# Emitting the first two mixer groups inside the last column chunk of a long convolution

## The chip, the cores, the metric

The kernel runs on one core of one Trainium2 chip. The metric is the device time of one execution in microseconds (us); lower is better. Each kernel ran several times, and the text quotes medians. A profile shows one further execution, whose span (first to last instruction) is a few us shorter than the timed runs.

The names of the engines in the profile are: PE is the tensor engine (TensorE), DVE is VectorE, ACT is ScalarE, POOL is GpSimd, SP is SyncE (here only a DMA queue). PEclk is the granted clock of TensorE; 1.00 is full speed.

## The reference, cut

Sequence length S = 2048, width D = 1024, MLP width F = 3584, all in bf16.

```python
def A(q, k, v, shift_k, ssm_k, ssm_D):
    kv = (4-tap causal filter of k with shift_k) * v
    y  = irfft(rfft(kv, 2*S) * rfft(ssm_k, 2*S))[:S] + kv * ssm_D   # long convolution over time
    return q * y
def B(x, w1, w2, w3, w4):
    h  = gelu(layernorm(x) @ w1)
    hs = (quarters of h shifted by +1, -1, +2, -2 in time) @ w2
    x1 = x + hs
    return x1 + gelu(layernorm(x1) @ w3) @ w4
x = q
for layer in range(2):
    x = x + A(layernorm(x), k, v, shift_k, ssm_k, ssm_D)
    x = x + B(layernorm(x), w1, w2, w3, w4)
```

The convolution's y depends on k, v and the filters only, not on x. So the kernel computes it once and uses it in both layers.

## The kernel before

**Stage 1** makes y, in four column chunks of 256 channels. In each chunk there are four blocks of time. For block c, TensorE transforms the filter block and the key-value block with a matrix `Fm` (ScalarE evicts them to `Gc`, `Xc`), VectorE makes the products of all pairs of blocks that add up to c (`Za`) and joins neighbours (`Wa`), and TensorE transforms back with `Im`. A store puts y into DRAM (`y_scr`). Block 2 has 3 pairs and block 3 has 4, so VectorE has most to do at the end of a chunk.

**Stage 2** runs 2 layers of 8 groups of 256 rows. For each group: `A_pre` (layer norm, times y, residual, second norm; VectorE with a `pow` on GpSimd), `A_tr` (transposes), `M1` (W1 and gelu), `M2` (W2 with the time shifts), `B_pre` (norm), `B_tr` (transposes), `M34` (W3, gelu, W4: 28 steps f; pieces of the next groups are hooked in at chosen f). "First down-projection" below is the first W4 matmul of group 0: from there on the tensor engine is the limit.

```python
with ExitStack() as p0:                         # stage 1
    cpool = ...                                 # Fm, Im
    with ExitStack() as g0:                     # scratch to compute Fm: kk, prod, pi, rf
        ...
    inp = p0.enter_context(tc.tile_pool(name="p0in", bufs=1))     # knat, hnat, v, kT
    blk, spec, zpool, tpool, wpool0, ypool = ...
    nxt0 = prep0(0)                             # loads k, ssm_k, v of a chunk
    for cc in range(NCH):
        for c in range(NB):
            ...forward transforms, products Za, Wa, inverse transforms...
            nc.gpsimd.dma_start(out=y_t[...], in_=ysb[:])
# p0 is closed here
with ExitStack() as p1:                         # stage 2: its own pools in p0's place
    w3_sb = w3p.tile([P, DT, F], BF16, name="w3_sb")              # 7 MB
    w4p = tile_pool(bufs=4); io = ...; xap = ...; small = ...
    def A_pre(g):
        x_t = io.tile([P, D], BF16, tag="x")
        nc.sync.dma_start(x_t[:], x_src[...])
        y_tile = io.tile([P, D], BF16, tag="y")
        nc.sync.dma_start(y_tile[:], y_scr[...])
        mv = stats(xs)
        nc.gpsimd.tensor_scalar(out=r1[:], in0=mv[:, :, 1], scalar1=EPS, ... op0=ALU.add)
        nc.gpsimd.tensor_tensor(out=r1[:], in0=r1[:], in1=mhalf[:, 0:TPC], op=ALU.pow)
        ...
    for i in range(-3, NG):
        hooks = {}
        ...                                     # W3 and W4 loads at i = -2, -1
        if ok(i + 2): M1(i + 2)                 # hooked at f = 4 when i is 0
        if ok(i + 3): add_hook(hooks, 0, A_pre(i + 3))
        if ok(i + 1): add_hook(hooks, 6 or 1, (M2(i + 1), B_pre(i + 1)))
        if ok(i + 1): add_hook(hooks, 14 or 10, B_tr(i + 1))
        if ok(i + 3): add_hook(hooks, 18, A_tr(i + 3))
        M34(i, hooks)                           # for i < 0: only the hooks, in order of f
```

Of the kernel before, what the change touches and what calls it, by code (L numbers as in the profile page):

```python
# [16 lines left out]
P = 128  # L17
EPS = 1e-5


def _layernorm(nc, small, mhalf, src, dst, D, norm_engine="act"):
    nchunks = (D + 511) // 512
    csz = D // nchunks
    st = small.tile([P, nchunks, 6], FP32, tag="ln_st")
    for i in range(nchunks):
        nc.vector.bn_stats(st[:, i, :], src[:, i * csz:(i + 1) * csz])
    mv = small.tile([P, 2], FP32, tag="ln_mv")
    nc.vector.bn_aggr(mv[:], st[:])
    rstd = small.tile([P, 1], FP32, tag="ln_rstd")
    nc.gpsimd.tensor_scalar(out=rstd[:], in0=mv[:, 1:2], scalar1=EPS, scalar2=None, op0=ALU.add)  # L30
    nc.gpsimd.tensor_tensor(out=rstd[:], in0=rstd[:], in1=mhalf[:], op=ALU.pow)
    if norm_engine == "act":
        nmr = small.tile([P, 1], FP32, tag="ln_nmr")
        nc.vector.scalar_tensor_tensor(out=nmr[:], in0=mv[:, 0:1], scalar=-1.0, in1=rstd[:],
                                       op0=ALU.mult, op1=ALU.mult)
        nc.scalar.activation(out=dst, in_=src, func=AF.Identity, bias=nmr[:], scale=rstd[:])
    else:
        nc.vector.tensor_scalar(out=dst, in0=src, scalar1=mv[:, 0:1], scalar2=rstd[:],
                                op0=ALU.subtract, op1=ALU.mult)
# [3 lines left out]
def kernel(ctx, tc, A_q, A_k, A_v, A_shift_k, A_ssm_k, A_ssm_D, B_x, B_w1, B_w2, B_w3, B_w4, out,  # L43
# [25 lines left out]

    y_scr = tc.dram_tile([S, D], BF16, name="y_scr")  # L70
    y_t = y_scr.rearrange("(t p) d -> p t d", p=P)

# [3 lines left out]
    ident1 = wts12.tile([P, P], BF16, name="ident1")  # L76
    make_identity(nc, ident1[:])
    mhalf = wts12.tile([P, 8], FP32, name="mhalf")
    nc.vector.memset(mhalf[:], -0.5)

    with ExitStack() as p0:
        cpool = p0.enter_context(tc.tile_pool(name="p0c", bufs=1))
        ident = ident1
        Fm = cpool.tile([P, KT, 2, Bs], FP32R, name="Fm")
# [3 lines left out]
        sgn = cpool.tile([P, 2], FP32, name="sgn")  # L88

        with ExitStack() as g0:  # L90
# [17 lines left out]
            for (dst, freev, pc) in ((Fm, kk, pcF),):  # L108
                for j in range(KT):
                    prod = gt.tile([P, 2, Bs], FP32, tag="prod")  # L110
                    nc.vector.tensor_scalar(out=prod[:, 0, :], in0=freev[:], scalar1=pc[:, j:j + 1],
                                            scalar2=float(3 * N // 2), op0=ALU.mult, op1=ALU.add)
                    nc.vector.tensor_scalar(out=prod[:, 1, :], in0=freev[:], scalar1=pc[:, j:j + 1],
                                            scalar2=None, op0=ALU.mult)
                    pi = gt.tile([P, 2, Bs], I32, tag="pi")
                    nc.vector.tensor_copy(pi[:], prod[:])
                    nc.vector.tensor_single_scalar(out=pi[:], in_=pi[:], scalar=2 * N - 1, op=ALU.bitwise_and)
                    rf = gt.tile([P, 2, Bs], FP32, tag="rf")
                    nc.vector.tensor_copy(rf[:], pi[:])
                    nc.scalar.activation(out=dst[:, j, :, :], in_=rf[:], func=AF.Sin, bias=negpi[:],  # L120
                                         scale=math.pi / N)

        inp = p0.enter_context(tc.tile_pool(name="p0in", bufs=1))
        blk = p0.enter_context(tc.tile_pool(name="p0blk", bufs=NB + 1))
        spec = p0.enter_context(tc.tile_pool(name="p0spec", bufs=4))
        zpool = p0.enter_context(tc.tile_pool(name="p0z", bufs=3))
        tpool = p0.enter_context(tc.tile_pool(name="p0t", bufs=3))
        wpool0 = p0.enter_context(tc.tile_pool(name="p0w", bufs=2))
        ypool = p0.enter_context(tc.tile_pool(name="p0y", bufs=2))
        ps_ks = p0.enter_context(tc.tile_pool(name="ps_ks", bufs=3, space=PSUM))  # L130
# [3 lines left out]
        def prep0(cc):  # L134
# [10 lines left out]
            for pc_ in range(npiece):  # L145
                tsl = slice(pc_ * tpp, (pc_ + 1) * tpp)
                nc.sync.dma_start(knat[:, tsl, :], k2.rearrange("(t p) d -> p t d", p=P)[:, tsl, ch0:ch0 + CC])
                nc.sync.dma_start(hnat[:, :, pc_ * tpp * P:(pc_ + 1) * tpp * P],
                                  A_ssm_k[ch0:ch0 + CC, pc_ * tpp * P:(pc_ + 1) * tpp * P].rearrange("(ct p) t -> p ct t", p=P))
                nc.sync.dma_start(v_sb[:, tsl, :], v2.rearrange("(t p) d -> p t d", p=P)[:, tsl, ch0:ch0 + CC])  # L150
# [50 lines left out]
        for cc in range(NCH):  # L201
# [4 lines left out]
            Zprev = None  # L206
            for c in range(NB):
# [19 lines left out]
                if cc == 0 and c == 0:  # L227
                    identf = cpool.tile([P, P], FP32, name="identf")
                    nc.vector.tensor_copy(identf[:], ident[:])
                    for comp in range(2):  # L230
                        for kt in range(KT):
                            pti = ps_fw.tile([P, KT, P], FP32, tag="fw")
                            for j in range(KT):
                                nc.tensor.transpose(pti[:, j, :], Fm[:, j, comp, kt * P:(kt + 1) * P].bitcast(FP32), identf[:])
                            nc.scalar.copy(Im[:, kt, comp, :], pti[:].rearrange("p a b -> p (a b)"))
                a = c
# [29 lines left out]
                for mp in range(KT // 2):  # L266
# [13 lines left out]
                    nc.gpsimd.dma_start(out=y_t[:, t0:t0 + 2, ch0:ch0 + CC], in_=ysb[:])  # L280
# [6 lines left out]
    TC = 256  # L287
    TPC = TC // P
    NCk = S // TC
    NG = 2 * NCk  # L290
    NH = D // 512
    QD = D // 4
    SHIFTS = [1, -1, 2, -2]
    HALO = 2
    nst = (D + 511) // 512
    csz = D // nst
    xa_scr = [tc.dram_tile([S, D], BF16, name=f"xa_scr{l}") for l in range(2)]
    xc_scr = tc.dram_tile([S, D], BF16, name="xc_scr")
    W4P = 4
    assert FT % W4P == 0  # L300
    NPC = FT // W4P
    W4SLOTS = 4

    with ExitStack() as p1:
        w3p = p1.enter_context(tc.tile_pool(name="w3p", bufs=1))
        w3_sb = w3p.tile([P, DT, F], BF16, name="w3_sb")
        w3v = B_w3.rearrange("(kt p) n -> p kt n", p=P)
        w4v = B_w4.rearrange("(kt p) n -> p kt n", p=P)
        W3PIECES = 7 if FT % 7 == 0 else 4
        fs3 = F // W3PIECES  # L310

        def w3_load(i):
            nc.sync.dma_start(w3_sb[:, :, i * fs3:(i + 1) * fs3], w3v[:, :, i * fs3:(i + 1) * fs3])
        w4p = p1.enter_context(tc.tile_pool(name="w4s", bufs=W4SLOTS))
        io = p1.enter_context(tc.tile_pool(name="io", bufs=2))
        xap = p1.enter_context(tc.tile_pool(name="xap", bufs=3))
        xbp = p1.enter_context(tc.tile_pool(name="xbp", bufs=3 * TPC))
        x1p = p1.enter_context(tc.tile_pool(name="x1p", bufs=2 * TPC))
        xlp = p1.enter_context(tc.tile_pool(name="xlp", bufs=2 * TPC))
        small = p1.enter_context(tc.tile_pool(name="small", bufs=6))  # L320
        atp = p1.enter_context(tc.tile_pool(name="aTp", bufs=2))
        btp = p1.enter_context(tc.tile_pool(name="bTp", bufs=2))
        hp = p1.enter_context(tc.tile_pool(name="hTp", bufs=3))
        up = p1.enter_context(tc.tile_pool(name="up", bufs=3))
        ps_s = p1.enter_context(tc.tile_pool(name="ps_side", bufs=2, space=PSUM))
        ps_3 = p1.enter_context(tc.tile_pool(name="ps_3", bufs=2, space=PSUM))
        ps_a = p1.enter_context(tc.tile_pool(name="ps_a", bufs=1, space=PSUM))

        def stats(src_list):
            n = len(src_list)  # L330
            mv = small.tile([P, n, 2], FP32, tag=f"mv{n}")
            for i, src in enumerate(src_list):
                st = small.tile([P, nst, 6], FP32, tag="ln_st")
                for j in range(nst):
                    nc.vector.bn_stats(st[:, j, :], src[:, j * csz:(j + 1) * csz])  # L335
                nc.vector.bn_aggr(mv[:, i, :], st[:])
            return mv

        def lc(g):
            return g // NCk, g % NCk  # L340

        st_aT = {}
        st_a = {}
        st_xb = {}
        st_hT = {}
        st_x1 = {}
        st_b = {}
        st_bT = {}

        def A_pre(g):  # L350
            layer, c = lc(g)
            x_src = q2 if layer == 0 else xc_scr
            xs = []
            ys = []
            for i in range(TPC):
                t = c * TPC + i
                x_t = io.tile([P, D], BF16, tag="x")
                nc.sync.dma_start(x_t[:], x_src[t * P:(t + 1) * P, :])
                y_tile = io.tile([P, D], BF16, tag="y")
                nc.sync.dma_start(y_tile[:], y_scr[t * P:(t + 1) * P, :])  # L360
                xs.append(x_t)
                ys.append(y_tile)
            mv = stats([x[:] for x in xs])
            r1 = small.tile([P, TPC], FP32, tag="r1")
            nc.gpsimd.tensor_scalar(out=r1[:], in0=mv[:, :, 1], scalar1=EPS, scalar2=None, op0=ALU.add)
            nc.gpsimd.tensor_tensor(out=r1[:], in0=r1[:], in1=mhalf[:, 0:TPC], op=ALU.pow)
# [178 lines left out]
        def ok(g):  # L545
            return 0 <= g < NG

# [61 lines left out]
```

## Time and profile before

The time is 1368.26 us (median of 6; 1365.24 to 1370.02).

| stretch of the trace | us | what limits it |
|---|---|---|
| start to first forward transform | 37.7 | TensorE waits for the first loads |
| start of the first forward transform to the end of the last | 217.1 | VectorE's products and TensorE together |
| end of the last forward transform to the first down-projection | 95.9 | VectorE in one chain with short TensorE work |
| first down-projection to the end | 1012.8 | TensorE |

The table of stretches of the kernel before: stretch, its length, busy us of each engine with the number of instructions, then clock, DMA share and GB/s.

```profile
core 0: us, PE busy (x) PEld busy (x) DVE busy (x) ACT busy (x) POOL busy (x), PEclk, DMA share, GB/s
254.80:350.70 95.90, 46.01 (x305) 36.75 (x306) 73.11 (x147) 16.93 (x36) 12.60 (x26) 0.72 0.59 198
350.70:1363.50 1012.80, 996.65 (x7060) 683.91 (x7182) 303.94 (x617) 241.44 (x611) 118.60 (x170) 1.00 0.44 148
```

In the transition TensorE is busy 46.0 of 95.9 us, at a mean clock of 0.72, and VectorE 73.1. From the first down-projection on, TensorE is busy 98%.

The timeline of TensorE in the transition, kernel before: start, us, engine, line, operation, out<-in, form, number, and in brackets the idle time just before it with what ended it.

```profile
260.29 2.08 PE L273 MATMUL ps<-Wa,Im 128*128 128x256 f32 x8 [5.47 <-DVE Wa L261]
...
280.84 5.53 PE L273 MATMUL ps<-Wa,Im 128*128 128x256 f32 x32 [13.10 <-DVE Wa L261]
297.90 1.95 PE L410 MATMUL pt<-ident,a_t 128*128 128x128 bf16 x16 [11.53 <-DVE a_t L400]
300.59 9.24 PE L424 MATMUL ps<-aT,w_sb 128*128 128x256 bf16 x64 [0.74 <-ACT aT L412]
313.85 0.62 PE L410 MATMUL pt<-ident,a_t 128*128 128x128 bf16 x8 [4.02 <-DVE a_t L400]
...
344.49 1.89 PE L477 MATMUL pt<-ident,b_t 128*128 128x128 bf16 x16 [13.13 <-DVE b_t L467]
```

One reads the brackets as the chain: TensorE waits for `Wa` twice, then for `a_t` of group 0 and group 1 (VectorE's norms), then for `b_t`. The W1 matmuls of group 0 take 9.24 us after the long wait; the same 64 take about 7.15 us at full clock.

### The profile page before, as it was taken

What the parts mean: (1) busy time and instruction counts of PE and PEld (TensorE: products, weight loads), DVE (VectorE), ACT (ScalarE), POOL (GpSimd) and SP (SyncE); (2) the same over time, 40 slices, a digit from 0 to 9 for tenths busy, and PEclk for the clock granted to TensorE, in tenths of its full rate; (3) what the DMA queues carried; (4) which work ended last, traced back from release to release, by engine and by line L of the source; (5) the groups of instructions that cost most, each with busy time, mean ns of one, the idle gap of its engine ahead of it and who ended that gap; (6) DMA issues with size and microseconds to landing.
All of it is one profiled execution on the core that took longest, in us unless ns stands there. A gap on an engine that the chain in (4) does not pass through costs nothing.

```text
span 1363.5 us, 22911 instructions
## 1 busy us (share of the span) xinstructions
PE 1268.4 (93%) x9635; PEld 940.3 (69%) x9760; DVE 586.0 (43%) x1103; ACT 404.1 (30%) x882; POOL 153.1 (11%) x233
## 2 busy tenths in 40 slices
PE   2999999635899999999999999999999999999997
PEld 2999999633666666676767666666666676766664
DVE  4479999985545151515151423324151512022000
ACT  4756555211222222231312222222222222311221
POOL 0001010111111021111111111101010210101011
PEclk9999999868899999999999999999999999999999
DMA  8330200466254544454444535353544443434441
GB/s 247 102 101 24 79 24 17 147 208 216 78 173 145 178 155 160 150 170 155 155 142 153 170 124 173 123 200 124 179 146 171 140 152 98 170 108 155 130 164 47
DMA packets 112783, 189.19 MB, mean 139 GB/s; under 512 B 6436, under 2 KB 31016, under 8 KB 112680
## 3 DMA queue, kind: packets, MB, share of 16 engines
q1 hardware_dynamic: 111144, 183.53, 40.9%
q0 software_dynamic: 1536, 4.20, 1.0%
q8 instruction: 76, 1.25, 0.4%
q14 instruction: 27, 0.22, 0.0%
HBM read 166.73 MB, written 20.97 MB: 138 GB/s over the span
## 4 chain that ended last, share of the span: by engine, by line
PE 78%; DVE 16%; issue 3%; POOL 1%; ACT 1%; DMA 0%; SPq 0%; POOLq 0%; DVEq 0%; ACTq 0%
PE ps L504 28%; PE acc L516 28%; PE ps L424 8%; PE ps L448 8%; DVE tmp L255 4%; DVE Za L256 4%; PE ps L221 1%; PE pt L410 1%; PE pt L477 1%; DVE Wa L261 1%; PE ps L273 1%; PE ps L191 1%; DVE kvb L194 1%; DVE Wa L263 1%; DVE st L335 1%
## 5 line engine op out<-in xcount | busy, mean ns | idle before, releaser
L504 PE MATMUL ps<-bT,w_sb 128*128 128x256 bf16 x3584 | 462.1, 273 | 0.0
L516 PE MATMUL acc<-wt,u 128*128 128x512 bf16 x1683 | 444.0, 379 | 7.2 <-DVE tmp L541 1.5
L504 PEld LDWEIGHTS <-w_sb 128*128 128x128 bf16 x3584 | 350.8, 98 | 131.7 <-issue 2.0
L507 ACT ACTIVATE u<-ps 128x256 bf16<-128x256 f32 x448 | 172.1, 384 | 686.0 <-PE ps L504 686.0
L516 PEld LDWEIGHTS <-u 128*128 128x128 bf16 x1792 | 174.1, 98 | 122.0 <-ACT u L507 2.6
L541 DVE TENSOR_TENSOR tmp<-acc,x 128x512 bf16<-128x512 f32 x64 | 42.7, 689 | 321.2 <-PE ps L504 201.9
L542 POOL TENSOR_TENSOR xa_t<-tmp,xa_t 128x512 bf16<-128x512 bf16 x64 | 71.7, 1154 | 557.7 <-DVE tmp L541 557.7
L424 PE MATMUL ps<-aT,w_sb 128*128 128x256 bf16 x1024 | 117.3, 276 | 1.5 <-ACT aT L412 1.4
L424 PEld LDWEIGHTS <-w_sb 128*128 128x128 bf16 x1024 | 101.6, 99 | 17.8 <-issue 2.1
L448 PE MATMUL ps<-w_sb,hTc 128*128 128x512 bf16 x496 | 110.2, 379 | 0.8
L273 PE MATMUL ps<-Wa,Im 128*128 128x256 f32 x512 | 70.3, 295 | 22.6 <-DVE Wa L261 21.7
L448 PEld LDWEIGHTS <-hTc 128*128 128x128 bf16 x512 | 50.1, 98 | 57.0
L273 PEld LDWEIGHTS ps<-Wa,Im 128*128 128x128 f32 x512 | 65.2, 200 | 26.3 <-issue 13.3
L400 DVE TENSOR_SCALAR a_t<-xa,rr,nbb 128x1024 bf16<-128x1024 bf16 x32 | 16.4, 543 | 153.7 <-PE pt L410 153.7
L451 DVE TENSOR_TENSOR x<-ps,xb 128x512 bf16<-128x512 f32 x64 | 43.9, 686 | 73.4 <-PE ps L448 72.4
L426 ACT ACTIVATE hTc<-ps 128x256 bf16<-128x256 f32 x128 | 49.2, 385 | 84.7 <-PE ps L424 84.7
L221 PE MATMUL ps<-h,Fm 128*128 128x256 f32 x512 | 66.4, 280 | 0.0
L256 DVE TENSOR_TENSOR Za<-Za,tmp 128x1024 bf16<-128x1024 bf16 x96 | 62.3, 675 | 0.0
L255 DVE TENSOR_TENSOR tmp<-Gc,Xc 128x1024 bf16<-128x1024 bf16 x96 | 62.3, 675 | 0.0
L221 PE MATMUL ps<-kvb,Fm 128*128 128x256 f32 x512 | 62.3, 277 | 0.0
L221 PEld LDWEIGHTS ps<-h,Fm 128*128 128x128 f32 x512 | 61.6, 188 | 0.4 <-ACT Gc L223 0.2
L221 PEld LDWEIGHTS ps<-kvb,Fm 128*128 128x128 f32 x512 | 60.1, 188 | 0.0
(83 smaller groups left out, 851.6 us busy)
## 6 DMA issues: line engine op xcount, KB each, us to landing
wt<-in_B_w_dram SPq DMA_DIRECT2D x112, 1024.0 KB, 5.4
y_tile<-y_scr SPq DMA_DIRECT2D x32, 256.0 KB, 3.7
xa_scr<-xa SPq DMA_DIRECT2D x32, 256.0 KB, 2.2
xa_t<-xa_scr SPq DMA_DIRECT2D x32, 256.0 KB, 2.7
w_sb<-in_B_w_dram SPq DMA_DIRECT2D x7, 1024.0 KB, 8.7
w_sb<-in_B_w_dram SPq DMA_DIRECT2D x2, 2048.0 KB, 13.4
y_scr<-ysb POOLq DMA_DIRECT2D x32, 128.0 KB, 2.2
x_t<-in_A_q_dram SPq DMA_DIRECT2D x16, 256.0 KB, 4.0
```

What stands on the lines that cost most here:

```text
L221: nc.tensor.matmul(ps[:, i, :], lhsT=Fm[:, j, comp, kt * P:(kt + 1) * P], rhs=src[:, j, :], start=(j == 0), stop=(j == KT - 1))
L255: nc.vector.tensor_tensor(out=tmp[:], in0=u, in1=w, op=ALU.mult)
L256: nc.vector.tensor_tensor(out=Za[:, comp, :], in0=Za[:, comp, :], in1=tmp[:], op=op)
L273: nc.tensor.matmul(ps[:, i, :], lhsT=Im[:, kt, comp, mt * P:(mt + 1) * P], rhs=Wa[:, comp, kt * CC:(kt + 1) * CC], start=(idx == 0), stop= ...
L424: nc.tensor.matmul(ps[:], lhsT=w1_sb[:, kt, m * P:(m + 1) * P], rhs=aT[:, kt, :], start=(kt == 0), stop=(kt == DT - 1))
L426: nc.scalar.activation(out=hTc[:, m, HALO:HALO + TC], in_=ps[:], func=AF.Gelu_apprx_tanh)
L448: nc.tensor.matmul(ps[:], lhsT=hTc[:, kt, c0:c0 + P], rhs=w2_sb[:, kt, nh * 512:(nh + 1) * 512], start=(kt == 0), stop=(kt == DT - 1))
L451: nc.vector.tensor_tensor(out=x1[:, nh * 512:(nh + 1) * 512], in0=ps[:], in1=xb[:, nh * 512:(nh + 1) * 512], op=ALU.add)
L504: nc.tensor.matmul(ps[:], lhsT=w3_sb[:, kt, f * P:(f + 1) * P], rhs=bT[:, kt, :], start=(kt == 0), stop=(kt == DT - 1))
L507: nc.scalar.activation(out=u[:], in_=ps[:], func=AF.Gelu_apprx_tanh)
L516: nc.tensor.matmul(acc[i][nh][:], lhsT=u[:, i * P:(i + 1) * P], rhs=wt[:, f % W4P, nh * 512:(nh + 1) * 512], start=(f == 0), stop=(f == FT ...
L542: nc.gpsimd.tensor_tensor(out=xal[i][:, sl], in0=tmp[:], in1=xal[i][:, sl], op=ALU.add)
```

## The change

Its intent is to fill the transition: mixer groups 0 and 1 need only x and y rows of blocks 0 and 1, which are ready while VectorE still makes the products of blocks 2 and 3 of the last chunk. So their work is emitted inside the last chunk. For this the pools of the two stages must live together: stage 2's tiles for x, y, the norms and the residuals become rings in the places of stage 1's tiles, and 2 of the 7 MB of W3 go into the place of `Fm`.

```diff
+    inp = ctx.enter_context(tc.tile_pool(name="p0in", bufs=1))      # now ahead of the Fm scratch
+    blk = ctx.enter_context(tc.tile_pool(name="p0blk", bufs=NB + 1))
+    fmw = ctx.enter_context(tc.tile_pool(name="fmw3", bufs=1))
+    def ring(name):            # x/y, xn/a, xa, b: in the places of knat, hnat, v, kT
+        tag = {"A": "knat", "B": "hnat", "C": "v", "D": "kT"}[name]
+        ...
+    def A_pre(g): ...          # the same arithmetic
-            nc.gpsimd.tensor_scalar(out=r1[:], in0=mv[:, :, 1], scalar1=EPS, ...)
+        nc.vector.tensor_scalar(out=ve1[:], in0=mv[:, :, 1], scalar1=EPS, ...)
     with ExitStack() as p0:
-        Fm = cpool.tile([P, KT, 2, Bs], FP32R, name="Fm")
+        Fm = fmw.tile([P, KT, 2, Bs], FP32R, tag="fmw", name="Fm")
         with ExitStack() as g0: ...
-        inp = p0.enter_context(tc.tile_pool(name="p0in", bufs=1))
-        tpool = p0.enter_context(tc.tile_pool(name="p0t", bufs=3))
+        tpool = p0.enter_context(tc.tile_pool(name="p0t", bufs=2))
         ...
+                if last and c == NB - 2:
+                    A_pre(0); A_tr(0); M1(0); A_pre(1); A_tr(1)
+                if last and c == NB - 1:
+                    w3e = fmw.tile([P, DT, W3E * P], BF16, tag="fmw", name="w3e")
+                    (two 1 MB loads of W3 into w3e)
+                    M1(1); M2(0); B_pre(0); B_tr(0)
                 ...products, Wa, inverse...
-                    nc.gpsimd.dma_start(out=y_t[...], in_=ysb[:])
+                    nc.scalar.dma_start(out=y_t[...], in_=ysb[:])
     with ExitStack() as p1:
-    W4SLOTS = 4
+    W4SLOTS = 3
+        A_pre(2)
-        for i in range(-3, NG):
+        for i in range(0, NG):
             ...
             if i == 0:         # group 0's M34 in manual order on TensorE;
+                A_tr(2) at f = 5, M1(2) at 7, M2(1) and B_pre(1) at 9, A_pre(3) at 10, B_tr(1) at 17, A_tr(3) at 22
```

The semicolons and the text in brackets shorten the diff. Left out are the moves of the other tiles of stage 2 into these rings, and the order of the remaining W3 and W4 loads, which are now issued ahead of `A_pre(2)` (W3 in pieces of 1 MB, as before).

## The prediction

> **What bounds it now.** The page gives the tensor engine (PE) 93% of the 1363.5 us span. The table of stretches places the rest: from 400 to 1360 us PE is busy 947.6 of 960 us (clock 1.00). From 254.8 us (last forward transform) to 350.7 us (first down-projection of group 0) it is busy 46.0 of 95.9 us, mean clock 0.72. There the vector engine (DVE) leads, 73.1 us busy. PE waits for Wa (13.1 us), a_t (11.5) and b_t (13.1). DVE finishes the products of the last 256 columns (282.6 us); only then come the layer norms of groups 0 and 1, W1, W2, the next norm.
>
> **What the change does.** Same arithmetic. Mixer groups 0 and 1 (A_pre, transposes, W1; W2 and B_pre for group 0) are emitted inside the last column chunk, among the products of blocks 2 and 3. 2 of 7 MB of W3 overlay the transform matrix and load early. Also: y stores issued by ACT instead of GpSimd; 3 W4 slots instead of 4; group 0 of the MLP in manual order.
>
> The instruction orders are the same on PE from MLP group 1 on: no gain there; a W4 piece serves about 7 us of PE and lands in 5.4, so 3 slots should suffice.
>
> **Cost in the transition**, laid out in the new order with the trace's durations (product 0.60 us, Wa 1.20, A_pre about 10.9 of DVE, power 0.72/1.03 plus about 0.6 handover, W1 7.0 warm, 9.2 cold, W2 7.1):
> - Block 2's products start at about 249.5 us.
> - a_t of group 0 at about 265 instead of 298; W1 ends near 277.
> - a_t of group 1 at about 283; Wa of block 2 near 287 and 290; W1 of group 1 to 300, W2 to 308.
> - DVE works off block 3's products between W2 evictions; last Wa at about 321 and 323 instead of 279.4 and 281.3.
> - The first W4 loads wait for exactly that last Wa (they overlay its inputs) and land at about 329; the last inverse transform ends near 328.
> - First down-projection at about 329 instead of 350.7. Less 1.9 (group 2's transposes, now later) and 0.5 waiting: **gain about 20 us**.
>
> DVE is idle only 22.8 of those 95.9 us, which caps the gain near there. PE gaps remain, so the clock stays partly low: the Trainium skill, "TensorE: Matmul & The Clock Gate", Part 1, says an idle window of about 3.4 us throttles PE to half rate; this trace agrees (W1 9.24 us after a gap, 7.15 warm).
>
> Moving the y stores is worth little: "DMA: Bandwidth & Descriptors", "Issuing engines are not separate DMA queues", says it saves only sequencer time. GpSimd's 23.4 us of issue are off the path; ACT, 60% busy in the transform stage, takes it on (0 to 4 us lost).
>
> **Prediction:** 1347 us (1338 to 1358). Faster by over 2%: 0.17; within 2%: 0.81; slower: 0.02.
>
> **Right if:** first down-projection near 329 us; PE idle before it down by about 20 us; last Wa later by about 40 us; DVE nearly gapless 250-323; MLP stage as long as before. **Wrong step if:** the transform stage lengthens (ACT evictions behind store issues), PE waits for W4 or W3 in group 0, or waits appear in groups 1 to 15 (3 slots, loads queued behind waiting ones).
>
> **What could break it:** handovers shorter or longer than my 0.5 us; the slow clock hitting W2 and the last inverse.

## More of the kernel before

At i = -1 the hooks run in order of f, so `A_pre(2)` (f = 0) comes before `M2(0)` and `B_pre(0)` (f = 1).

From the page of the kernel before, first part and slices: the busy line of the engines (busy us, share of the span, number of instructions), then TensorE's busy share in 40 equal slices (9 is 90% or more) and its clock in tenths.

```profile
PE 1268.4 (93%) x9635; PEld 940.3 (69%) x9760; DVE 586.0 (43%) x1103; ACT 404.1 (30%) x882; POOL 153.1 (11%) x233
...
PE   2999999635899999999999999999999999999997
...
PEclk9999999868899999999999999999999999999999
```

The first slice (34 us) is only 2 tenths busy, and slices 8 to 10 (from about 239 us) are 6, 3 and 5 tenths busy: two dips, one at the start and one in the transition. In all others but the last (7 tenths) TensorE is busy 8 tenths or more.

The timeline of the start of the kernel before: the first key load on the SP queue, and TensorE's first transpose and first forward transform.

```profile
14.91 0.39 SPq L147 DMA_DIRECT2D knat<-in_A_k_dram  x1
...
17.96 0.59 PE L168 MATMUL ptk<-ident,knat 128*128 128x128 bf16 x4 [17.96 <-DMA knat<-in_A_k_dram]
...
37.66 2.53 PE L221 MATMUL ps<-h,Fm 128*128 128x256 f32 x20
```

The key load is issued at 14.91 us.

## The result, and the profile after

The changed kernel takes 1328.18 us (median of 8; 1326.51 to 1329.2), against 1367.5 us beside it. The ratio is 0.9711, 95% interval [0.9701, 0.9721]: 2.9% faster, where at most 2.2% was in the range. A ratio here is the mean time of one kernel's fast runs over that of the other's of the same rounds, so it is not quite the ratio of the medians quoted. Where I turn a ratio r into us below, it is (1 − r) × 1367.5; the whole gain is then 39.5 us.

From the page of the changed kernel, the same lines:

```profile
PE 1271.9 (96%) x9635; PEld 942.7 (71%) x9760; DVE 592.8 (45%) x1167; ACT 404.8 (31%) x883; POOL 113.2 (9%) x121
...
PE   6999999768999999999999999999999999999997
...
PEclk9999999889999999999999999999999999999999
```

Both dips are shallower: the first slice is 6 tenths busy (2 before), and slices 8 to 10 are 7, 6 and 8 tenths (6, 3 and 5 before).

The table of stretches of the changed kernel, from the start of its last forward transform (243.03 us; it ends at 247.0) to the first down-projection and from there to the end:

```profile
core 0: us, PE busy (x) PEld busy (x) DVE busy (x) ACT busy (x) POOL busy (x), PEclk, DMA share, GB/s
243.00:312.40 69.40, 46.15 (x321) 35.83 (x321) 65.04 (x131) 17.67 (x37) 5.23 (x5) 0.83 0.32 103
312.44:1326.00 1013.56, 997.80 (x7076) 684.89 (x7199) 321.79 (x698) 243.12 (x614) 105.52 (x106) 1.00 0.48 158
```

The last stretch is as long as before (1013.6 against 1012.8 us), so the gain lies wholly ahead of the first down-projection. That one comes at 312.44 us in place of 350.70: 38.3 us earlier. The first line here begins 4 us too early to be set beside the 95.9 us above: counted from the end of the last forward transform, as there, the transition takes 65.4 us, with VectorE busy 61.1 us and TensorE's mean clock at 0.82.

The timeline of TensorE in the transition, changed kernel (names differ: `ringB` holds `a_t`, `ringD` holds `b_t`):

```profile
253.28 1.95 PE L191 MATMUL pt_a<-ident,ringB 128*128 128x128 bf16 x16 [6.29 <-DVE ringB L179]
255.96 8.86 PE L204 MATMUL ps_m<-aT,w_sb 128*128 128x256 bf16 x64 [0.74 <-ACT aT L192]
269.79 1.95 PE L191 MATMUL pt_a<-ident,ringB 128*128 128x128 bf16 x16 [4.98 <-DVE ringB L179]
272.48 4.21 PE L204 MATMUL ps_m<-aT,w_sb 128*128 128x256 bf16 x19 [0.74 <-ACT aT L192]
...
285.14 7.07 PE L227 MATMUL ps_m<-w_sb,hTc 128*128 128x512 bf16 x31
297.53 1.89 PE L263 MATMUL pt_b<-ident,ringD 128*128 128x128 bf16 x16 [5.33 <-DVE ringD L247]
...
306.38 3.09 PE L476 MATMUL ps<-Wa,Im 128*128 128x256 f32 x24 [1.21 <-DVE Wa L466]
312.44 1.02 PE L556 MATMUL acc<-wt,u 128*128 128x512 bf16 x3 [2.97 <-DMA wt<-in_B_w_dram]
```

The waits for `a_t` are 6.29 and 4.98 us (before 11.53 and 4.02), the one for `b_t` 5.33 (before 13.13), and there is a new one of 2.97 us for the first W4 piece. Of the long waits for `Wa` (5.47 and 13.10 us before) 1.21 us is left. `M2(0)` follows `M1(1)` without a wait.

The timeline of the start, changed kernel:

```profile
1.64 0.39 SPq L331 DMA_DIRECT2D knat<-in_A_k_dram  x1
...
4.52 0.61 PE L353 MATMUL ptk<-ident,knat 128*128 128x128 bf16 x4 [4.52 <-DMA knat<-in_A_k_dram]
...
27.04 4.02 PE L407 MATMUL ps<-h,Fm 128*128 128x256 f32 x32
```

The first key load is issued 13.3 us earlier, and the first forward transform starts 10.6 us earlier. This is ahead of anything that was interleaved.

Set against the prediction, in us from the start of the span:

| event | before | predicted | after |
|---|---|---|---|
| `Wa` of block 1, first half, starts | 243.3 | | 234.7 |
| block 2's products of the last chunk start | 245.1 | 249.5 | 238.95 |
| transposes of `a_t(0)` | 297.9 | 265 | 253.3 |
| transposes of `a_t(1)` | 313.85 | 283 | 269.8 |
| `M1(1)` ends | 324.5 | 300 | 285.3 |
| last `Wa` ready | 282.6 | about 323 | 306.3 |
| first down-projection | 350.7 | 329 | 312.4 |

Counted from block 2's products, the last `Wa` was predicted after 73.5 us and came after 67.4. So of the 16.6 us by which the first down-projection came earlier than predicted, 10.5 were already there when these products began, and 6.1 came between them and the last `Wa`; the last leg, from `Wa` to the down-projection, was as predicted (6 us predicted, 6.1 measured). Of the 10.5 us, 8.65 were there at the first half of `Wa` of block 1, where the interleaving has put no more than two statistics instructions of group 0 so far; they come from the start.

Of the prediction's own checks, VectorE was nearly gapless, as it said (busy 63.3 of the 67.4 us). The last `Wa` came 23.7 us later than before, where it said about 40. TensorE stood idle 38.4 us before the first down-projection, against 78.9: 40.6 us less, where it said about 20.

### The profile page after: what moved, and what is told of

It reads as the page before. It is cut to its first block, busy times and chain, and to the rows that moved or that the text cites. A ratio compares the mean times of both kernels' runs of the same rounds, so it can differ in the third digit from the quotient of the medians.

```text
span 1326.0 us, 22848 instructions
## 1 busy us (share of the span) xinstructions
PE 1271.9 (96%) x9635; PEld 942.7 (71%) x9760; DVE 592.8 (45%) x1167; ACT 404.8 (31%) x883; POOL 113.2 (9%) x121
## 4 chain that ended last, share of the span: by engine, by line
PE 80%; DVE 16%; DMA 1%; issue 1%; POOL 1%; SPq 0%; ACT 0%; POOLq 0%; DVEq 0%
PE ps L544 29%; PE acc L556 29%; PE ps_m L204 8%; PE ps_m L227 8%; DVE tmp L458 4%; DVE Za L459 4%; PE ps L407 1%; PE ps L476 1%; PE ps L376 1%; PE pt_a L191 1%; PE pt_b L263 1%; DVE Wa L464 1%; DVE kvb L379 1%; DVE Wa L466 1%; DVE st L103 1%
## 5 line engine op out<-in xcount | busy, mean ns | idle before, releaser
L544 PE MATMUL ps<-bT,w_sb 128*128 128x256 bf16 x2560 | 331.8, 273 | 0.0
L544 PEld LDWEIGHTS <-w_sb 128*128 128x128 bf16 x2560 | 250.5, 98 | 97.3
L583 DVE TENSOR_TENSOR ringD<-acc,x1p 128x512 bf16<-128x512 f32 x64 | 42.7, 689 | 307.5 <-PE ps L544 186.6
L544 PE MATMUL ps<-bT,w3e 128*128 128x256 bf16 x1024 | 131.8, 275 | 1.0 <-DVE bT L264 1.0
L544 PEld LDWEIGHTS <-w3e 128*128 128x128 bf16 x1024 | 100.9, 99 | 36.2 <-issue 3.2
L204 PE MATMUL ps_m<-aT,w_sb 128*128 128x256 bf16 x1024 | 118.4, 278 | 1.5 <-ACT aT L192 1.5
L584 POOL TENSOR_TENSOR xa_t<-ringD,xa_t 128x512 bf16<-128x512 bf16 x64 | 71.7, 1154 | 544.8 <-DVE ringD L583 541.0
L204 PEld LDWEIGHTS <-w_sb 128*128 128x128 bf16 x1024 | 101.8, 100 | 18.0 <-issue 1.8
L227 PE MATMUL ps_m<-w_sb,hTc 128*128 128x512 bf16 x496 | 110.2, 379 | 0.8
L230 DVE TENSOR_TENSOR x1p<-ps_m,xbp 128x512 bf16<-128x512 f32 x64 | 44.0, 687 | 78.6 <-PE ps_m L227 77.7
L206 ACT ACTIVATE hTc<-ps_m 128x256 bf16<-128x256 f32 x128 | 49.2, 385 | 86.9 <-PE ps_m L204 86.9
```

What stands on the lines that cost most here:

```text
L204: nc.tensor.matmul(ps[:], lhsT=w1_sb[:, kt, m * P:(m + 1) * P], rhs=aT[:, kt, :], start=(kt == 0), stop=(kt == DT - 1))
L206: nc.scalar.activation(out=hTc[:, m, HALO:HALO + TC], in_=ps[:], func=AF.Gelu_apprx_tanh)
L227: nc.tensor.matmul(ps[:], lhsT=hTc[:, kt, c0:c0 + P], rhs=w2_sb[:, kt, nh * 512:(nh + 1) * 512], start=(kt == 0), stop=(kt == DT - 1))
L230: nc.vector.tensor_tensor(out=x1p[:, j, nh * 512:(nh + 1) * 512], in0=ps[:], in1=xbp[:, j, nh * 512:(nh + 1) * 512], op=ALU.add)
L544: nc.tensor.matmul(ps[:], lhsT=w3_tile(kt, f), rhs=bT[:, kt, :], start=(kt == 0), stop=(kt == DT - 1))
L584: nc.gpsimd.tensor_tensor(out=xal[i][:, sl], in0=tmp, in1=xal[i][:, sl], op=ALU.add)
```

## The experiments

All kernels gave correct results. The expectations call "theory A" that the part of the gain which the prediction lacked comes from the early first loads and the rest from the interleaving; its rivals are named there. The time of the kernel before, beside these runs, was 1365.2 to 1368.7 us.

### 1. Only the early first loads: `early_inputs`

The kernel before, with one pool allocated ahead of the scratch for `Fm`:

```diff
+        inp = p0.enter_context(tc.tile_pool(name="p0in", bufs=1))
         with ExitStack() as g0:
             ...
-        inp = p0.enter_context(tc.tile_pool(name="p0in", bufs=1))
```

> The kernel before, with one line moved: the pool of the first inputs is allocated before the scratch of the trigonometric tables, so that it no longer overlays it. Theory A (the prediction missed that the change also takes the first loads out of a wait for that scratch; worth the 10.2 us by which the vector engine's chain leads in the trace of after): first key transposes near 4.5 instead of 18 us, first forward transform near 27 instead of 37.7 us, time about 1357 us (ratio 0.9925). Theory B (all of the gain is made in the transition, the early lead is eaten by the vector engine's backlog or by DMA queueing): within 2 us of the kernel before, ratio above 0.998.

Measured: 1355.08 us, ratio 0.9912 [0.9893, 0.993], so 12.0 us off. In the timeline of its start:

```profile
1.62 0.39 SPq L147 DMA_DIRECT2D knat<-in_A_k_dram  x1
...
28.62 4.02 PE L221 MATMUL ps<-h,Fm 128*128 128x256 f32 x32
```

The loads no longer wait for the scratch whose bytes they lie in. In the kernel before, a pool opened after the scratch pool was closed got the same bytes, and the first loads on the SP queue had to wait until ScalarE had read the last scratch tile (to write `Fm`). From the waits of the SP queue in the kernel before: line, what it waited for, us in total, times, longest.

```profile
SPq L141 <- ACT Fm L120: 12.2, 1, 12.2
```

In the traces the first forward transform comes 9.0 us earlier than before (28.62 against 37.66), and the first down-projection also 9.0 us (341.70 against 350.70); the 12.0 us by the ratio (interval 9.6 to 14.6) lie above that. The profiled execution of the kernel before was the fastest of its six, and that of `early_inputs` the slowest of its four. One moved line is worth between a quarter and a third of the whole gain.

### 2. The other way round: `late_inputs`

The changed kernel, with the first of the four pieces of each first load held by one-column copies out of the last column of `Fm`:

```diff
+            if cc == 0:
+                last_trig = Fm[:, KT - 1, 1, Bs - 1:Bs]
+                for held in (knat[:, 0, 0:1], hnat[:, 0, 0:1], v_sb[:, 0, 0:1]):
+                    nc.vector.tensor_copy(held, last_trig)
```

> The changed kernel, with the first loads of k, v and the filter held back until the trigonometric table is written (a one-column copy from the table into each tile, overwritten by the load), as they were before. Theory A: about 10 us are lost, near 1338 us (ratio 0.978), and first down-projection near 322 instead of 312.4 us. Theory B: 1328 to 1330 us, no loss.

Measured: 1337.77 us, ratio 0.9786 [0.9768, 0.9804]; against 0.9711 that is 10.3 us lost, and the first down-projection comes at 322.47 us, 10.0 later. The two runs agree from both sides: the early loads are worth 9 to 12 us, and this lead is not used up later.

### 3. The changed kernel without the interleaving: `no_overlap`

```diff
-                if last and c == NB - 2:
-                    A_pre(0); A_tr(0); M1(0); A_pre(1); A_tr(1)
                 ...
-                    M1(1); M2(0); B_pre(0); B_tr(0)
+        # after the chunk loop, in the old order
+        A_pre(0); A_tr(0); M1(0); A_pre(1); A_tr(1); M1(1); M2(0); B_pre(0); B_tr(0)
```

> The changed kernel, but the work of groups 0 and 1 (norms, W1, W2, next norm) is emitted after the last column chunk instead of inside it; early loads, shared pools, stores on ACT, three W4 slots stay. Theory A: the early lead of 10 us stays and the transition's 26 us are lost: 1354 us (ratio 0.990), last Wa near 271 us, first down-projection near 340. Theory B (everything is the transition): back to 1365 or more. A rival to the overlap itself (shared pools and the early 2 MB of W3 make the gain, not the interleaving): stays below 1340 us.

Measured: 1343.5 us, ratio 0.983 [0.9806, 0.9853]. The expectation failed by 10 us: the interleaving by itself is worth 16.3 us (0.983 − 0.9711), not the whole rest. Between this kernel and `early_inputs` (0.9912) lie 11.2 us that are neither the start nor the interleaving. Experiments 5 to 9 look for them.

### 4. A part of the interleaving: `w2_after`

The changed kernel, but `M2(0)`, `B_pre(0)`, `B_tr(0)` come after the last chunk:

```diff
                 if last and c == NB - 1:
                     ...
                     M1(1)
-                    M2(0); B_pre(0); B_tr(0)
+        M2(0); B_pre(0); B_tr(0)      # after the chunk loop
```

> The changed kernel, but only W2, the norm after it and its transposes for group 0 are emitted after the last column chunk. The vector engine's total is the same, so if that engine is the chain through the transition, the last Wa comes about 7 us earlier (near 299), the W4 wait of 3 us disappears, and the first down-projection stays within 3 us of 312.4: 1326 to 1331 us. If instead PE is the chain (W2 7 us, transposes 2, cold clock), 7 to 10 us are lost: 1335 to 1338 us.

Measured: 1329.46 us, ratio 0.9724 [0.9706, 0.9743], 1.8 us lost. The last `Wa` is ready at 299.8 us here, 6.5 earlier, because VectorE does the W2 evictions and the `b_t` norm after it; the first down-projection is at 315.78 us, 3.3 later (3 were allowed). The 7 to 10 us that TensorE as the chain would have cost did not come. This fits a chain in which VectorE's sum of work counts from the products to the down-projection, and where that work stands among the products shifts the end only by a few us; experiment 11 tests it by taking work away.

### 5. The short GpSimd chain: `early_eps`

`early_inputs`, with the additions of eps on VectorE, as in the changed kernel, so that GpSimd does one `pow` alone:

```diff
-            nc.gpsimd.tensor_scalar(out=rr[:, 0, :], in0=mv[:, :, 1], scalar1=EPS, ...)
-            nc.gpsimd.tensor_scalar(out=rr[:, 1, :], in0=rr[:, 0, :], scalar1=EPS, ... op0=ALU.mult)
-            nc.gpsimd.tensor_tensor(out=rr[:, 1, :], in0=rr[:, 1, :], in1=mv[:, :, 1], op=ALU.add)
+            nc.vector.tensor_scalar(out=rr[:, 0, :], ...)
+            nc.vector.scalar_tensor_tensor(out=rr[:, 1, :], ...)
             nc.gpsimd.tensor_tensor(out=rr[:], ..., op=ALU.pow)
```

> The first kernel with the early first loads (1355.1 us) and, in addition, the eps and variance additions on VectorE, so that the GpSimd chain is one pow. If the shorter handover to GpSimd in group 0 and 1 lies on the chain (about five handovers of about 1 us each): 1350 to 1351 us. Rival, that these handovers are hidden behind other waits of VectorE: 1354 to 1356 us.

Measured: 1354.74 us, ratio 0.9914 [0.9899, 0.9928], which is the ratio of `early_inputs`: no gain that the intervals show. The timelines of VectorE show why the 4 to 5 us were a miscount. First `early_inputs`, then `early_eps`:

```profile
287.93 0.23 DVE L390 SCALAR_TENSOR_TENSOR nbb<-mv,rr 128x2 f32<-128x2 f32 x2 [2.07 <-POOL rr L386]
```

```profile
284.23 0.17 DVE L383 TENSOR_SCALAR rr<-mv 128x2 f32<-128x2 f32 x1
284.43 0.16 DVE L384 SCALAR_TENSOR_TENSOR rr<-rr,mv 128x2 f32<-128x2 f32 x1
285.76 0.23 DVE L390 SCALAR_TENSOR_TENSOR nbb<-mv,rr 128x2 f32<-128x2 f32 x2 [1.17 <-POOL rr L386]
```

The wait is 0.9 us shorter, but VectorE now has the two additions itself, which with their starts take about 0.4 us. What is left, 0.7 us by the transposes of `a_t(0)` (16.4 us after the last inverse transform's start, against 17.1), was lost again: W1 of group 1 took 9.65 us here and 8.01 in `early_inputs`, at a lower clock. A gain of less than a us ahead of a TensorE gap can vanish in it.

### 6. The place of group 2's norm: `early_group2_late`

`early_inputs`, with `A_pre(2)` after `B_tr(0)` as the changed kernel has it:

```diff
-                add_hook(hooks, 0, A_pre(i + 3))
+                add_hook(hooks, 10 if i == 0 else 11 if i == -1 else 0, A_pre(i + 3))
             # A_tr(2) moves into M34(0) at f = 5; the other hooks of group 0, and the manual order
             # of its M34 on TensorE, as in the changed kernel
```

> The first kernel with the early first loads (1355.1 us), and A_pre of group 2 placed after B_pre and B_tr of group 0, its transposes inside the gate projections of group 0. If group 2's statistics and the wait for its x load stood in front of b_t of group 0 (TensorE waited 13.1 us for b_t before, about 5 in the changed kernel): about 1347 us. Rival, that VectorE has the same sum of work and the wait only moves to a later place: 1354 to 1356 us.

Measured: 1350.15 us, ratio 0.9883 [0.9866, 0.9901]: 4.0 us beyond `early_inputs` by the ratios (4.9 by the medians), less than the 8 expected, but the mechanism shows. From the timelines, `early_inputs` first (VectorE waits for x of group 2, then TensorE for `b_t` of group 0), then `early_group2_late`:

```profile
312.46 1.29 DVE L335 BATCH_NORM_STATS2 st<-x_t 128x6 f32<-128x512 bf16 x2 [6.51 <-DMA x_t<-in_A_q_dram]
...
335.75 1.89 PE L477 MATMUL pt<-ident,b_t 128*128 128x128 bf16 x16 [13.15 <-DVE b_t L467]
```

```profile
325.24 1.89 PE L477 MATMUL pt<-ident,b_t 128*128 128x128 bf16 x16 [4.63 <-DVE b_t L467]
```

The statistics of group 2 stood in front of `b_t(0)` in VectorE's order, with a wait of 6.51 us for their x load. Moving them takes 8.5 us off the wait for `b_t`, and the first down-projection comes 8.8 us earlier (332.86 against 341.70). Some 1.9 us go back, since the transposes of group 2 now stand inside `M34(0)` (from the first down-projection to the end: 1014.9 us, 1013.0 before). That leaves 6.9 us between the profiled spans (1354.7 and 1347.8), and 4 to 5 between the timed runs. The difference is a matter of which execution was profiled: that of `early_inputs` was the slowest of its four (1356.47 us), that of `early_group2_late` the fastest (1349.62). The manual order, which comes with this edit, is not what shortened the wait for `b_t`: `M34(0)` stands after that wait in TensorE's order.

### 7. Both edits: `early_eps_late`

The edits of experiments 5 and 6 together, on `early_inputs`.

> Both of the two edits on top of the early first loads. If these two and the early loads are all that the changed kernel has besides the interleaving: equal to the changed kernel without the interleaving, 1343.5 us (1341 to 1346). If something else is in the changed kernel (loads that no longer wait for pools), this stays at 1348 us or above.

Measured: 1349.3 us, ratio 0.9875 [0.986, 0.989]. It stays 6.2 us above `no_overlap` (0.983). So something else is in the changed kernel. The timelines, first of `early_eps_late`, then of `no_overlap`, show where:

```profile
269.30 0.35 SPq L358 DMA_DIRECT2D x_t<-in_A_q_dram  x1
...
274.32 0.69 DVE L335 BATCH_NORM_STATS2 st<-x_t 128x6 f32<-128x512 bf16 x1 [0.60 <-DMA x_t<-in_A_q_dram]
...
289.80 1.29 DVE L335 BATCH_NORM_STATS2 st<-x_t 128x6 f32<-128x512 bf16 x2 [1.97 <-DMA x_t<-in_A_q_dram]
...
302.81 0.62 PE L410 MATMUL pt<-ident,a_t 128*128 128x128 bf16 x8 [4.08 <-DVE a_t L400]
...
305.43 9.48 PE L424 MATMUL ps<-aT,w_sb 128*128 128x256 bf16 x64 [0.67 <-ACT aT L412]
```

```profile
162.64 0.82 SPq L138 DMA_DIRECT2D ringA<-in_A_q_dram  x2
...
299.06 0.62 PE L191 MATMUL pt_a<-ident,ringB 128*128 128x128 bf16 x8 [1.37 <-DVE ringB L179]
...
301.33 7.15 PE L204 MATMUL ps_m<-aT,w_sb 128*128 128x256 bf16 x64 [0.74 <-ACT aT L192]
```

In the first, `early_eps_late`, x of group 0 is issued at 269.30 us. The waits of the SP queue name VectorE's `tmp` (22.1 us in one wait): stage 2's pools lie in the bytes of stage 1's, and the load has to wait until the last of the products is made. VectorE then waits for x of both groups (0.60 and 1.97 us). TensorE's wait for `a_t(1)` is 4.08 us, and W1 of group 1 runs 9.48 us. In `no_overlap` x of group 0 is issued at 162.64 us, that of group 1 at 280.32 (282.37 in `early_eps_late`), VectorE waits for neither, TensorE's wait is 1.37 us, and W1 takes 7.15 us. This is where the clock enters: the Trainium skill, "TensorE: Matmul & The Clock Gate", Part 1, puts the idle window after which the clock halves at about 3.4 us. The trace agrees on both sides of it: after 1.37 us W1 still runs at 112 ns per matmul (7.15 / 64), and in the changed kernel after 4.98 us the first 19 take 222 ns each (4.21 / 19). A short wait for a load can thus cost 2.3 us more than itself. The loss is not fixed by the wait alone: after 4.03 us in `early_inputs` the same W1 took 8.01 us.

### 8. Late x loads alone: `no_overlap_late_x`

`no_overlap`, with the x loads of groups 0 and 1 held by one-column copies into their ring:

```diff
+                if last and a == NB - 1:      # after the last product of component 0
+                    rA0 = ring("A")
+                    for i in range(TPC):
+                        nc.vector.tensor_copy(rA0[:, i, 0:1], Za[:, 0, 0:1])
...
+        if g == 0:                            # after the second norm's variance of group 0
+            for i in range(TPC):
+                nc.vector.tensor_copy(rA[:, i, 0:1], ve2[:, 0, 0:1])
```

> The changed kernel without the interleaving (1343.5 us), whose x loads of groups 0 and 1 are held, by one-column copies into their tile, until about the points at which the first kernel with early loads, short GpSimd chain and late group 2 issued them (after the last product of the last block; after the second norm of group 0). If the x loads of the two groups explain the 6 us by which that kernel (1349.3 us) is longer: 1348 to 1350 us, VectorE waiting for both x loads again, and W1 of group 1 at the low clock again (9.5 us, 7.15 in the kernel without the interleaving). Rival, that the remainder lies in the weights' loads or the stores: 1343 to 1345 us.

Measured: 1344.88 us, ratio 0.9832 [0.9818, 0.9845]; the rival's range. From its timeline:

```profile
271.86 0.82 SPq L138 DMA_DIRECT2D ringA<-in_A_q_dram  x2
...
301.35 0.62 PE L194 MATMUL pt_a<-ident,ringB 128*128 128x128 bf16 x8 [1.35 <-DVE ringB L182]
...
303.62 7.15 PE L207 MATMUL ps_m<-aT,w_sb 128*128 128x256 bf16 x64 [0.74 <-ACT aT L195]
```

Issued as late as 271.86 us (group 0) and 285.41 us (group 1), x still landed in time: median 2.9 us from issue to landing, where in `early_eps_late` it was 5.8. So the theory, as I had put it, fell: the late issue alone does not do it.

### 9. Late x loads in company: `no_overlap_late_loads`, `no_overlap_late_all`

What differs is the company. In `early_eps_late` all of stage 2's pools come free at the same time, so x, y and W3 are issued one behind the other. The Trainium skill, "DMA: Bandwidth & Descriptors", "Queues, rings and completion order", says that the DMA engines take descriptors in ring order. So I expected a 256 KB load of x behind a 1 MB piece of W3 on the same queue to land late. The kernel `no_overlap_late_loads` holds y and the first two W3 pieces as well:

```diff
+                nc.vector.tensor_copy(rA0[:, 2 + i, 0:1], Za[:, 0, 0:1])         # y of group 0
+            nc.vector.tensor_copy(rA[:, 2 + i, 0:1], ve2[:, 0, 0:1])             # y of group 1
+            w3e_piece(0, nb1[:, 0:1])         # first W3 piece: after the first norm of group 0
+            w3e_piece(1, xas[1][:, 0:1])      # second: after xa of group 0
```

`no_overlap_late_all` is the same with the y stores on GpSimd (the edit of experiment 10).

> As the run before (1344.9 us, with the x loads of groups 0 and 1 issued late), and the y loads of both groups and the first two W3 pieces held too, so that x loads share the queue with y and W3 loads, as in the first kernel with its two edits. If it is the company of the other loads that made x late there: the x loads take 4 to 8 us to land (2.9 in the run before), VectorE waits for x of group 1 about 2 us, and 1347 to 1350 us in all. Rival, that even so the loads land in time: 1344 to 1346 us.

> The same with the y stores issued from GpSimd. If a store that GpSimd issues stands in front of the pow of group 0's first norm (VectorE waited 1.69 us for it in the first kernel with its edits, 0.83 otherwise), about 1 us more than the run above. Rival: no difference.

Measured: 1352.08 us, ratio 0.9882 [0.9866, 0.9899], and 1352.2 us, ratio 0.9884 [0.9869, 0.9899]. From the timeline of `no_overlap_late_loads`:

```profile
276.65 0.69 DVE L103 BATCH_NORM_STATS2 st<-ringA 128x6 f32<-128x512 bf16 x1 [0.81 <-DMA ringA<-in_A_q_dram]
...
293.90 1.28 DVE L103 BATCH_NORM_STATS2 st<-ringA 128x6 f32<-128x512 bf16 x2 [4.42 <-DMA ringA<-in_A_q_dram]
...
306.91 1.94 PE L199 MATMUL pt_a<-ident,ringB 128*128 128x128 bf16 x16 [6.46 <-DVE ringB L187]
309.60 8.56 PE L212 MATMUL ps_m<-aT,w_sb 128*128 128x256 bf16 x64 [0.74 <-ACT aT L200]
```

The waits for x are back, and W1 of group 1 is at the low clock in part. The loss against `no_overlap` is 7.1 us, where 6.2 were to be explained; it overshoots, probably because x of group 1 was held too long: it was issued 2.3 us ahead of the transposes of `a_t(0)`, 4.6 in `early_eps_late`, and the wait is 4.42 us against 1.97. x took 4.1 us to land and W3 9.3 us (medians), against 2.9 us for x alone; this agrees with what that page says of the order, but does not prove it, for in every slice from 277 to 298 us the DMA engines moved 308 to 403 GB/s, and a plain sharing of their bandwidth would delay x too. So the cause of the 6 us is shown in kind: x held late alone costs 1.4 us by the medians and nothing that the ratios show, x held late together with y and W3 brings the waits and the loss back. Its size is only near (7.1 against 6.2 us), and whether y or W3 does more was not tried. In the changed kernel the shared rings and the early 2 MB of W3 let most of these loads go out before the rush. The place of the stores has no part in it (0.1 us between the medians of the two runs).

### 10. Two parts thought harmless: `stores_on_gpsimd`, `before_3slots`

```diff
# the changed kernel
-                    nc.scalar.dma_start(out=y_t[...], in_=ysb[:])
+                    nc.gpsimd.dma_start(out=y_t[...], in_=ysb[:])
# the kernel before
-    W4SLOTS = 4
+    W4SLOTS = 3
```

> The changed kernel with the y stores issued from GpSimd again, as before. Theory: which engine issues them doesn't matter, 1328 us within 2. Rival: stores on the ScalarE queue are what makes the forward matmuls 5 per cent slower (3.96 us for 32 against 3.79); then that group goes back to 3.79, and the time may move by up to 3 us.

> The first kernel with three W4 slots in place of four, as the changed kernel has. If the fourth slot was never needed: the same time as the first kernel, within 0.2 per cent. Rival, that a slot less costs in every group: over 1370 us.

Measured: 1328.13 us, ratio 0.972 [0.9706, 0.9735], against 1328.18 us of the changed kernel; and 1367.03 us, ratio 1.0005 [0.999, 1.0021], the time of the kernel before. Both parts cost and gain nothing in the whole time that these runs can show, as predicted. The Trainium skill, "DMA: Bandwidth & Descriptors", "Issuing engines are not separate DMA queues", agrees: the issuing engine changes only its own sequencer's time. The first run also rejects the rival on the forward matmuls: their mean stays at 283 and 282 ns (280 and 277 in the kernel before). Why they are 1 to 2% longer in the changed kernel stays open; 1024 of them come to some 4 us of TensorE, at a place where VectorE leads. From the first forward transform to `Wa` of block 1 in the last chunk it took 207.65 us, 205.7 before. Of these 2 us the stores on ScalarE account for 0.8 to 0.9: the stretch is 206.82 us in `stores_on_gpsimd`, and 207.19 against 206.29 us in the two kernels of experiment 9, which differ in the stores alone. Two of group 0's statistics instructions, which VectorE already did there, account for less than their 1.3 us: kernels that differ in having them or not differ by 0.2 to 0.5 us (207.53 in `no_overlap` against 207.30 in `no_overlap_late_x`; 206.82 in `stores_on_gpsimd` against 206.29). The 0.8 us do not reach the end: the first down-projection is at 312.38 us in `stores_on_gpsimd`, 312.44 in the changed kernel.

### 11. Two further steps: `act_norms`, `w4_early`, `both`

If VectorE is the chain from the products to the last `Wa`, taking work from it must help. `act_norms` is the changed kernel with the normalised copies of groups 0 and 1 and the first two `bT` copies on ScalarE:

```diff
-            nc.vector.tensor_scalar(out=a_t, in0=xas[i], scalar1=rr[:, 1, i:i + 1], scalar2=nbb[:, 1, i:i + 1], ...)
+            nc.scalar.activation(out=a_t, in_=xas[i], func=AF.Identity, scale=rr[:, 1, i:i + 1], bias=nbb[:, 1, i:i + 1])
             # the same for xb, emitted after the transposes' copies; only for g < 2
```

`w4_early` loads the first W4 piece into the second half of the place of `Fm`, in place of the second early W3 piece (W3 then lies in pools of single pieces, and its loads alternate with W4's); `both` has both edits:

```diff
-                    w3e = fmw.tile([P, DT, W3E * P], BF16, tag="fmw", name="w3e")     # two W3 pieces
+                    early_w = fmw.tile([P, 2, W4P * D], BF16, tag="fmw", name="early_w")
+                    # half 0: first W3 piece, half 1: first W4 piece
```

> The changed kernel with the normalised x and b copies of groups 0 and 1 on ScalarE in place of VectorE. If VectorE's order of work is the chain from the block-2 products to the last Wa: about 5 us off, 1323 us. Rival, that TensorE at its cold clock or the first W4 load is the chain there: under 2 us, 1326 to 1329 us.

> The changed kernel with the first W4 piece loaded early into the place where the second half of the early W3 stood. The wait of 2.97 us of TensorE for W4 after the last inverse goes: first down-projection at about 309.6 in place of 312.4, 1325.5 us. Rival, that the wait only moves to a later load: 1327 to 1329 us.

> act_norms and w4_early together. If both theories hold, their gains add: about 8 us off, 1320 us. If the chain is elsewhere, not below 1326 us.

Measured: `act_norms` 1322.75 us, ratio 0.9679 [0.9665, 0.9693]; `w4_early` 1325.73 us, ratio 0.9705 [0.9691, 0.9719]; `both` 1322.17 us, ratio 0.9675 [0.9661, 0.969]. The first did what the VectorE theory expected (5.4 us between the medians, 4.4 by the ratios, beyond the intervals). The gain of the second is 2.4 us between medians, but 0.8 us by the ratios and within their intervals, so it is not shown, although the wait for W4 is gone. `both` beats the kernel before by 3.2% and the changed one by 0.4%, but it is not measurably better than `act_norms`: no second gain shows on top of the first. From the timelines of `act_norms`, then of `w4_early`:

```profile
268.24 0.62 PE L197 MATMUL pt_a<-ident,ringB 128*128 128x128 bf16 x8 [0.73 <-ACT ringB L179]
...
307.38 1.04 PE L567 MATMUL acc<-wt,u 128*128 128x512 bf16 x4 [0.84 <-ACT u L558]
```

```profile
311.49 1.04 PE L566 MATMUL acc<-early_w,u 128*128 128x512 bf16 x4 [0.96 <-ACT u L557]
```

With `act_norms` the last `Wa` is ready at 300.75 us, and the wait for the W4 piece is gone by itself: TensorE, which now is in the low clock with the last inverse transform and the first gate projections (mean 0.66 from 300 to 306 us), needs longer than the load. So there was nothing left for the early load to save.

## Why the prediction was wrong

The time was predicted at 1347 us and measured at 1328.2, outside the range. By the ratios, the gain of 39.5 us has these parts (each a difference of ratios times 1367.5; by the intervals each is good to about 3 us):

| part | us | shown by |
|---|---|---|
| first loads not behind the `Fm` scratch | 12.0 | 1, 2 |
| group 2's norm after `b_t(0)`; short GpSimd chain (about 0) | 5.1 | 5, 6, 7 |
| x, y and W3 not all issued at once | 6.2 | 7, 9 |
| groups 0 and 1 among the products | 16.3 | 3 |

The traces split the 38.3 us by which the first down-projection comes earlier in the same order, with less weight on the first part: 350.70 us before, 341.70 in `early_inputs`, 333.99 in `early_eps_late`, 327.43 in `no_overlap`, 312.44 in the changed kernel, so 9.0, 7.7, 6.6 and 15.0 us (of the 7.7 us, 1 to 2 go back later, as experiment 6 says).

Point by point:

- **"Block 2's products start at about 249.5 us."** This is the step that failed. It carried over the times of stage 1 from the trace of the kernel before. The products start at 238.95. The change moved the input pool ahead of the scratch, and the diff shows that line; the prediction treated stage 1 as unchanged but for ScalarE's stores ("0 to 4 us lost") and looked for all of the gain in the transition. Of the 16.6 us error in the first down-projection, 10.5 are this one term: 8.65 the lead from the start. The other 1.9 are what it put in there too much: it has these products start 4.4 us later than before, and group 0's statistics ahead of them took 2.5. That stage 1 itself loses 0 to 4 us was right: it lost 2.0, 0.8 to 0.9 of them by the stores on ScalarE, the reason that it gave.
- **The layout of the transition, 73.5 us from the products to the last `Wa`,** was right in its order and wrong in the size of its terms: 67.4 measured. It ran ahead little by little: 1.2 us by `a_t(0)`, 2.7 by `a_t(1)`, 4.2 at the end of W1 of group 1, 6.1 at the last `Wa`. From `a_t(1)` to the end of W1 of group 1 it allowed 17 us, and 15.5 were taken (only the first 19 of the 64 matmuls ran at the low clock). It counted each power on GpSimd with its own 0.72 or 1.03 us and a handover of 0.6; in the trace VectorE ran a product or a statistic in the meantime and stood idle 0.59 to 0.90 us at each, 4.05 us in all of the 67.4.
- **"DVE is idle only 22.8 of those 95.9 us, which caps the gain near there."** The cap was wrong. It held VectorE's work in that stretch fixed, but the place of the norms made some of it leave the stretch: about half of the norm of group 2 (6 us), and the first 5 us of group 3's, now lie under the MLP stage. From the end of the last forward transform to the first down-projection VectorE was busy 73.1 us before and 61.1 after, and idle 22.8 and 4.4: of the 30.4 us that this stretch lost, 18.4 were idle time and 12.0 work that left.
- **Last leg.** "The first W4 loads wait for exactly that last Wa" was right: TensorE waited 2.97 us for W4, and the leg took 6.1 us where 6 were predicted.
- **MLP stage "as long as before"** was right (1012.8 and 1013.6 us), and three W4 slots cost nothing (`before_3slots`).
- **Stores** were right: 0.8 to 0.9 us within stage 1, no effect on the time (`stores_on_gpsimd`).
- **The clock.** The rule was right and cuts both ways: it was the reason for some of the cost expected, and shorter waits won back clock as well as time (mean clock of the transition 0.72 before, 0.82 after).

## What to carry to other kernels

When a change moves pools, look at each tile that lands in other bytes, not only at the code that the change is about: what had to wait for the old tenant of those bytes, and when is the first load issued now? Ask for the issue time of the first load and compare it with the time at which its data could have been asked for. A cap on a gain, taken from an engine's idle time in one stretch, holds only if no work can leave that stretch; and two edits that shorten the same wait need not add up.

## What the Trainium skill lacked or had wrong

- "TensorE: Matmul & The Clock Gate", Part 1: nothing wrong. The runs agree with its window: full clock after an idle time of 1.37 us, half rate after 4.98 us (222 ns against 112 ns per matmul). The page also says that the window is free-running, so that the number of slow matmuls differs from run to run; the runs show how much that is here: the 64 matmuls of W1 of group 1 took 7.15 us after an idle time of 1.37 us, and 8.01 to 9.96 us after 4.0 to 4.5 us (`early_inputs`, `before_3slots`). A prediction needs that spread.
- "DMA: Bandwidth & Descriptors": its "Queues, rings and completion order" gives the order but no size for what a small load pays behind large ones. The runs show 2.9 us (median) for 256 KB of x issued apart from y and W3, 4.1 to 5.8 us with them beside it.
- "DMA: Bandwidth & Descriptors", "Issuing engines are not separate DMA queues": agrees (1328.13 and 1328.18 us). Nothing lacking or wrong.
- No page says why forward matmuls of the same shape take a mean of 283 and 282 ns in the changed kernel and 280 and 277 in the first. The runs leave it open; the stores' engine is not the reason.
